# Attention whose probabilities meet v unnormalised: the row sums' reciprocals are applied to a pair's output

## The chip, the cores and the metric

The program runs on one core of a Trainium2 chip. The metric is the time of one execution in device microseconds, the median of three runs of the kernel before: 1122.89 us (1122.71 to 1123.68). Of the engines, PE (TensorE) multiplies and transposes, DVE (VectorE), ACT (ScalarE) and POOL (GpSimd) work elementwise, and SP (SyncE) issues the DMAs. Each takes its own instructions in order.

## The reference, cut to what matters

For 4 batches of 8 heads (S = 576 positions, D = 64 columns) attention with a decay is computed, and its output goes through two MLPs:

```
scores = q @ k.T / 8 + decay                    # masked above the diagonal
attn = exp(scores - max);  attn /= sum(attn) + 1e-9
x = attn @ v                                    # heads side by side: 2304 rows of 512
x = leaky(x @ w_in) @ w_out                     # 2048 wide
x = ((x @ w_a) * (x @ w_b)) @ w_o               # 1536 wide
```

## The kernel before

Attention runs in 34 steps `u`, one for each of the 32 heads and two to drain. In step `u` the scores of head `u` are made, head `u-1` is turned into P (its probabilities, transposed), and head `u-2` is multiplied with v (`LAG` = 2). Two heads, an even one and the odd one behind it, are a pair `g`: they fill the 128 partitions of x together. The first 512 query rows of a head are four row tiles `i` of 128 rows (names `sc_n_i`, 128 to 512 columns by the causal mask); the last 64 rows of both heads of a pair are one more tile, called r (`scr`, `sr`), made in the odd step.

The softmax of a tile is one DVE instruction (L354: mask, minimum) and one ACT instruction (L355: exp with the row sums `sm`). `rinv` makes `ri` = 32768/sum of the four tiles on DVE (`PSCALE` = 2^15).

There are two ways to P. Heads 0 to 9 (`NATIVE`) stay in float32: POOL multiplies each tile by `ri` in place (`p_hi`, L396), PE transposes it against the identity (`transposed`, L418), ACT or DVE copies the result out of PSUM, and `pv_whole` (L467) multiplies. Heads 10 to 31 are split in two float16 parts: POOL writes hi = s * ri (L409), DVE writes lo = s * ri - hi (L489), four tiles each, and a DMA transposes the tiles of a group ("lo": tiles 0 and 1, "hi": 2 and 3, "r") into `PT`. `pv` (L511 to L513) multiplies. Its output is put together by ACT (L544) and DVE (L545), and x is split into xh (ACT, L207) and xl (POOL, L551) for the first MLP.

In steps from 10 on, the first seven of sixteen column blocks of the first MLP (`mlp1a`, tiles h, g, y; `leaky` on ACT, DVE and POOL) are laid between attention's instructions, where the tables `even` and `odd` have an M. The y tiles are copied to `ys` (L686, two buffers) and stored to `ya_d`. Behind attention come the rest of the first MLP in passes (hb, ya) and the second MLP (a, b, o).

PSUM has eight banks: three for the MLP tiles and five (`at`) that go round among scores, transposes and pv. When attention has ended, they become four and four. The tables `even0`, `odd0` (first ten steps), `even` and `odd` give the order in which a step's parts are written; a scheduler then orders each engine's instructions by its own estimate.

Of the kernel before, what the change touches and what calls it, by code (L numbers as in the profile page):

```python
# [19 lines left out]
T = B * S  # L20
# [32 lines left out]
    eng0={'h3': 'pool', 'U': 'pool', 'h1': 'pool', 'e0': 'act', 'e2': 'act', 'e3': 'dve', 'e4': 'dve'},  # L53
    even0=['ri', 's3', 'T', 'p0', 'h2', 'h3', 's2', 'vs', 'h1', 's0', 'Q', 'M', 'M', 'M', 'M', 'l1', 'l2', 'h0', 's1', 'l0', 'l3', 'p1', 'V', 'po', 'W', 'M'],
    odd0=['ri', 'h3', 'h2', 'h0', 'R', 'h1', 'rr', 'M', 'Q', 'l2', 'T', 'l3', 'M', 's3', 'h4', 's2', 'l1', 'l0', 'M', 'M', 's1', 's0', 'p0', 'vs', 'p1', 'V', 'W', 'po', 'l4', 'M'],
# [21 lines left out]
def decay_attention_then_two_mlps(ctx, tc, q, k, v, f, w_in, w_out, alpha, w_a, w_b, w_o, out):  # L77
# [308 lines left out]
    def p_hi(n, i):  # L386

        g, o = GROUP[i]
        if n < NATIVE:
            s = s_view(n, i)  # L390
            ri = ap_["rir"][:, 0:1] if i == 4 else ap_["ri", n % 2][:, i:i + 1]
            e = eng(f"h{i}", "pool")
            if e is act:
                act.activation(s, s, AF.Copy, scale=ri)
            else:
                e.tensor_scalar(s, s, ri, 1.0, op0=ALU.mult, op1=ALU.mult)  # L396
            return
        if (n, g) not in p16:
            p16[n, g] = ap_["a"].tile(
                [128, GSIZE[g], 128], F16, tag=f"p16_{g}", name=f"p16_{n}_{g}", bufs=_P.get("p16", {}).get(g, 1),  # L400
            ), []
        t = p16[n, g][0][:, o:o + 2 * i + 2]
        s = s_view(n, i).rearrange("p (t n) -> p t n", n=128)
        ri = ap_["rir"][:, 0:1] if i == 4 else ap_["ri", n % 2][:, i:i + 1]
        e = eng(f"h{i}", "pool")
        if e is act:
            act.activation(t[:, 0::2, :], s, AF.Copy, scale=ri)
        else:
            e.tensor_scalar(t[:, 0::2, :], s, ri, 1.0, op0=ALU.mult, op1=ALU.mult)  # L409
        p16[n, i] = t, s, ri  # L410
# [73 lines left out]
    def p_lo(n, i):  # L484
        if n < NATIVE:
            return p_whole(n, i)
        t, s, ri = p16.pop((n, i))
        g, o = GROUP[i]
        eng(f"l{i}", "dve").scalar_tensor_tensor(t[:, 1::2, :], s, ri, t[:, 0::2, :], op0=ALU.mult, op1=ALU.subtract)  # L489
        whole, done_ = p16[n, g]  # L490
        done_.append(i)
        if g == "r" or len(done_) == 2:
            PT[n, g] = ap_["a2"].tile(
                [128, GSIZE[g], 128], F16, tag=f"PT_{g}", name=f"PT_{n}_{g}", bufs=2 if g == "r" else LAG,
            )
            sp.dma_start_transpose(out=PT[n, g], in_=whole.rearrange("p t n -> p (t n)"))
            del p16[n, g]

    def pv(u, c):
# [36 lines left out]
        x32 = xs[g, c]
        x = x32[p0:p0 + 64]
        if eng("x", "dve") is pool:
            y = ap_["a"].tile([128, 256 + SR], F32, tag="y", name=f"y_{u}_{c}")[p0:p0 + 64, :w]
            act.activation(x, ps_o[p0:p0 + 64, :w], AF.Copy, scale=1.0 / PSCALE)  # L540
            act.activation(y, ps_o[o0:o0 + 64, :w], AF.Copy, scale=1.0 / PSCALE)
            pool.tensor_tensor(x, x, y, op=ALU.add)
        else:
            act.activation(x, ps_o[o0:o0 + 64, :w], AF.Copy, scale=1.0 / PSCALE)  # L544
            dve.scalar_tensor_tensor(x, ps_o[p0:p0 + 64, :w], 1.0 / PSCALE, x, op0=ALU.mult, op1=ALU.add)  # L545
        if j == 0:
            return
        x_tiles(b)
        xh, xl = (x_[:, hp, h0:h0 + w] for x_ in X[b])
        dup(eng("xh", "act"), xh, x32)  # L550
        eng("xl", "pool").tensor_tensor(xl, x32, f32(xh), op=ALU.subtract)  # L551
# [388 lines left out]
```

## Time and profile before

| | |
|---|---|
| time, median of 3 runs | 1122.89 us (1122.71 to 1123.68) |
| the profiled execution | 1123.5 us, span 1121.5 us |
| PE busy | 1069.1 us, 95% of the span |
| DVE, ACT, POOL busy | 565.5, 524.4, 491.9 us |
| PE clock granted, mean | 0.993 |

The span is the time from the first to the last instruction of the profiled execution. A busy engine is one whose instructions run; a wait is idle time in front of an instruction, put down to what ended it. Neighbouring matmuls overlap, so the time from start to start is what one costs in a row of them.

### The profile page before, as it was taken

The page shows a single profiled execution, that of the slowest core. Times are in us where ns is not written, and L with a number is a line of the kernel's source. Part 1 is how long each engine was busy: PE and PEld are TensorE (multiplying, and loading weights), DVE is VectorE, ACT ScalarE, POOL GpSimd, SP SyncE. Part 2 cuts the span into 40 slices and gives each one's busy share as a digit, 9 for nine tenths or more (in the row PEclk, how much of TensorE's full clock was granted, in tenths as well). Part 3 has the DMA queues.
Part 4 walks back from the last instruction along what each step waited for, and adds up shares of the span by engine and source line. Part 5 has one row for each costly group of instructions (what it writes and reads, how often), then busy time and mean ns, then how long its engine had stood idle before and what let it go on. Part 6 is the DMA issues. An engine that isn't in the chain of part 4 may idle for free.

```text
span 1121.5 us, 18956 instructions
## 1 busy us (share of the span) xinstructions
PE 1069.1 (95%) x6663; PEld 1001.4 (89%) x6663; DVE 565.5 (50%) x1360; ACT 524.4 (47%) x1407; POOL 491.9 (44%) x627
## 2 busy tenths in 40 slices
PE   5899999998999999999998999999999999999997
PEld 3767888888888989999998999999999999999997
DVE  5688979888888286877588445400000000000000
ACT  5776776777777465666555444321121111211211
POOL 5555767667677355555556654311111111111111
PEclk9999999999999999999999999999999999999999
DMA  4645366767874764887778873120110100200000
GB/s 109 160 133 183 79 140 127 188 141 125 197 142 88 207 214 136 283 264 228 258 243 291 290 255 101 51 85 1 42 44 1 57 29 1 85 1 1 29 1 28
DMA packets 210771, 141.24 MB, mean 126 GB/s; under 512 B 138420, under 2 KB 196788, under 8 KB 210676
## 3 DMA queue, kind: packets, MB, share of 16 engines
q1 hardware_dynamic: 210676, 140.03, 44.7%
q8 instruction: 52, 0.85, 0.3%
q14 instruction: 43, 0.35, 0.1%
HBM read 88.30 MB, written 33.65 MB: 109 GB/s over the span
## 4 chain that ended last, share of the span: by engine, by line
PE 60%; DVE 4%; DMA 2%; POOL 1%; issue 1%; ACT 1%; SPq 0%; DVEq 0%; POOLq 0%; ACTq 0%
PE a L646 5%; PE b L646 5%; PE a L645 5%; PE b L644 5%; PE b L645 5%; PE a L644 5%; PE o L644 4%; PE o L645 4%; PE o L646 4%; PE ya L645 3%; PE ya L644 3%; PE hb L644 3%; PE hb L646 3%; PE ya L646 3%; PE hb L645 3%
## 5 line engine op out<-in xcount | busy, mean ns | idle before, releaser
L910 DVE TENSOR_TENSOR as<-b,as 128x384 f32<-128x384 f32 x72 | 40.1, 557 | 367.6 <-PE b L646 366.7
L912 POOL TENSOR_TENSOR gg<-as,gg 128x384 fp32r<-128x384 f32 x72 | 73.2, 1017 | 334.9 <-ACT gg L911 334.9
L909 ACT COPY as<-a 128x384 f32<-128x384 f32 x72 | 34.6, 480 | 170.9 <-PE a L646 170.8
L911 ACT CAST gg<-as 128x384 fp32r<-128x384 f32 x72 | 36.9, 513 | 152.4 <-DVE as L910 152.3
L639 DVE SCALAR_TENSOR_TENSOR lt<-lu,nal,lt 128x288 f32<-128x288 f32 (+1 forms) x110 | 75.6, 688 | 54.5 <-ACT lt L638 53.9
L646 PE MATMUL a<-yh,w_a 128*128 128x384 f32 x288 | 97.2, 338 | 0.0
L646 PE MATMUL b<-yh,w_b 128*128 128x384 f32 x288 | 97.1, 337 | 0.0
L645 PE MATMUL a<-yl,w_a 128*128 128x384 f32 x288 | 97.1, 337 | 0.0
L644 PE MATMUL b<-yh,w_b 128*128 128x384 f32 x288 | 97.1, 337 | 0.0
L645 PE MATMUL b<-yl,w_b 128*128 128x384 f32 x288 | 97.1, 337 | 0.0
L644 PE MATMUL a<-yh,w_a 128*128 128x384 f32 x288 | 97.1, 337 | 0.0
L644 PE MATMUL o<-w_o,gg 128*128 128x512 f32 x216 | 84.4, 391 | 0.0
L645 PE MATMUL o<-w_o,gg 128*128 128x512 f32 x216 | 84.4, 391 | 0.0
L646 PE MATMUL o<-w_o,gg 128*128 128x512 f32 x216 | 84.2, 391 | 0.0
L355 ACT ACTIVATE s<-s,nm 128x512 f32<-128x512 f32 (+3 forms) x128 | 71.5, 560 | 22.9 <-DVE nm L354 22.2
L641 POOL TENSOR_TENSOR gb<-lt,gb 128x384 fp32r<-128x384 f32 x54 | 56.5, 1047 | 41.8 <-ACT gb L640 36.0
L645 PE MATMUL ya<-gb,w_out 128*128 128x384 f32 x216 | 73.3, 339 | 1.0 <-POOL gb L641 1.0
L644 PE MATMUL ya<-gb,w_out 128*128 128x384 f32 x216 | 71.3, 340 | 2.4 <-DVE yl L837 2.3
L646 PE MATMUL ya<-gb,w_out 128*128 128x384 f32 x216 | 72.9, 337 | 0.0
L645 PE MATMUL y<-g,w_out 128*128 128x288 f32 x224 | 69.2, 312 | 3.4 <-POOL g L641 3.4
L644 PE MATMUL y<-g,w_out 128*128 128x288 f32 x224 | 67.1, 312 | 2.5 <-ACT g L640 2.5
L644 PE MATMUL h<-xh,w_in 128*128 128x288 f32 x224 | 67.3, 303 | 1.5 <-ACT lt L638 1.1
(185 smaller groups left out, 3228.1 us busy)
## 6 DMA issues: line engine op xcount, KB each, us to landing
yl<-ya_d SPq DMA_DIRECT2D x48, 192.0 KB
wr_in<-in_moe_w_in SPq DMA_DIRECT2D x32, 256.0 KB
wr_out<-in_moe_w_out SPq DMA_DIRECT2D x32, 256.0 KB
wr_a<-in_moe_w_a SPq DMA_DIRECT2D x24, 256.0 KB
wr_b<-in_moe_w_b SPq DMA_DIRECT2D x24, 256.0 KB
wr_o<-in_moe_w_out SPq DMA_DIRECT2D x24, 256.0 KB
qkn<-in_q SPq DMA_DIRECT2D x64, 72.0 KB
qkn<-in_k SPq DMA_DIRECT2D x64, 72.0 KB
```

The costliest lines, as they stand in the source:

```text
L355: act.activation(s, s, AF.Exp, bias=nm, scale=-1.0, accum_out=sm)
L639: dve.scalar_tensor_tensor(t, u, nal[:, fi:fi + 1], t, op0=ALU.mult, op1=ALU.add)
L641: pool.tensor_tensor(gl, t, f32(gh), op=ALU.subtract)
L644: pe.matmul(o, lh, rh, start=start, stop=False)
L645: pe.matmul(o, lh, rl, start=False, stop=False)
L646: pe.matmul(o, ll, rh, start=False, stop=stop)
L909: act.copy(asb[:, :n], aps[:, :n])
L910: dve.tensor_tensor(asb[:, :n], bps[:, :n], asb[:, :n], op=ALU.mult)
L911: ap_["last"] = act.copy(g[:, 0, :n], asb[:, :n]).ins
L912: pool.tensor_tensor(g[:, 1, :n], asb[:, :n], f32(g[:, 0, :n]), op=ALU.subtract)
```

## The change

P is no longer multiplied by the reciprocal of its sum in row tiles 0 to 3. The reciprocals of a pair are spread by a DVE copy over 64 columns per head (`rinv_pair`), turned into rows by four PE transposes of 128x128 into one `at` bank (`rinv_rows`, new entry `rl` of the odd tables), copied by ACT into the one buffer `rrow`, and x of the pair is multiplied by `rrow`: in native heads as DVE reads the PSUM tile, in the others by one POOL instruction of 128x576 in x's only buffer. xh and xl are made once per pair, 576 columns wide. Tile r keeps its multiplication by `rir`. hi and lo are made by two instructions per head instead of four (`SPAN`: tiles 0 and 1 lie side by side as "lo", 384 columns, and tiles 2 and 3 as "hi", 896 columns), and native tiles 0 to 3 have no multiplication. `ys` goes from two buffers to one. The tables change; of them a line stands here.

```
-    odd="ri h3 h2 h0 R rr vs h1 M Q l2 T l3 s2 M h4 s3 l1 M M s1 l0 s0 p0 p1 V W po l4 M".split(),
+    odd="rl h1 h0 ri R rr vs M Q l1 T s2 M h4 s3 l0 M M s1 s0 p0 p1 V W po l4 M".split(),
...
+        ap_["rrow"] = a.tile([128, S], F32, name="rrow")
+        pool.memset(ap_["rrow"][:, ST:], 1.0 / PSCALE)
...
+    def rinv(sm, ri, scale):
+        dve.tensor_scalar(sm, sm, 1e-9, scale, op0=ALU.add, op1=ALU.mult)
+        if len(ri.shape) == 3:
+            dve.reciprocal(sm, sm)
+            dve.tensor_copy(ri, sm.unsqueeze(2).broadcast_to([128, 4, D]))
...
+    def rinv_pair(n):
+        g, j = divmod(n, 2)
+        if g not in RI:
+            RI[g] = ap_["a"].tile([128, 4, 2, D], F32, tag="ri", name=f"ri_{g}")
+        return RI[g][:, :, j]
+
+    def rinv_rows(g):
+        o = bank(f"rrow_{g}")
+        ri = RI.pop(g)
+        for i in range(4):
+            w = ri[:, i].rearrange("p j d -> p (j d)")
+            pe.transpose(o[:, 128 * i:128 * i + 128], w, ap_["ident"])
+        act.copy(ap_["rrow"][:, 0:ST], o)
...
+    SPAN = {0: ("lo", 0, 384), 1: ("hi", 384, 1280), 4: ("r", 0, 640)}
...
+    def p_hi(n, r):
         if n < NATIVE:
+            if r == 4:
+                s = ap_["sr"]
+                pool.tensor_scalar(s, s, ap_["rir"][:, 0:1], 1.0, op0=ALU.mult, op1=ALU.mult)
             return
+        g, s, scale = p_parts(n, r)
+        t = p16[n, r] = ap_["a"].tile([128, GSIZE[g], 128], F16, tag=f"p16_{g}", name=f"p16_{n}_{g}")
+        eng(f"h{r}", "pool").tensor_scalar(t[:, 0::2], s, scale, 1.0, op0=ALU.mult, op1=ALU.mult)
...
-        act.activation(xh, ps_o[:, :w], AF.Copy, scale=1.0 / PSCALE)
-        dve.scalar_tensor_tensor(xl, ps_o[:, :w], 1.0 / PSCALE, f32(xh), op0=ALU.mult, op1=ALU.subtract)
+        cs = slice(256 * c, 256 * c + w)
+        dve.tensor_tensor(x_pair(g)[:, cs], ps_o[:, :w], ap_["rrow"][:, cs], op=ALU.mult)
+        if c == 1:
+            x_out(g)
+
+    def x_pair(g):
+        if g not in xs:
+            xs[g] = ap_["a"].tile([128, S], F32, tag="x32", name=f"x32_{g}")
+        return xs[g]
+
+    def x_out(g):
...
+        dup(eng("xh", "act"), xh, x)
+        eng("xl", "pool").tensor_tensor(xl, x, f32(xh), op=ALU.subtract)
...
+        act.copy(x, ps_o[o0:o0 + 64, :w])
+        dve.tensor_tensor(x, ps_o[p0:p0 + 64, :w], x, op=ALU.add)
+        if j == 1 and c == 1:
+            eng("xr", "pool").tensor_tensor(xs[g], xs[g], ap_["rrow"], op=ALU.mult)
+            x_out(g)
...
-                ys = mp["t"].tile([128, HB], F32, tag="ys", name=f"ys_{b}_{a0}_{e_}")
+                ys = mp["t"].tile([128, HB], F32, tag="ys", bufs=1, name=f"ys_{b}_{a0}_{e_}")
```

On DVE, where head 30 is turned into P (step 31; `p16_30` are its float16 parts, `x32_14` the output of pair 14, `lt_2` a leaky of the MLP), there stood before:

```order
L377 TENSOR_SCALAR sm_0_152<-sm_0_152 128x4
L378 RECIPROCAL ri_0_153<-sm_0_152 128x4
L545 SCALAR_TENSOR_TENSOR x32_14_0_4991<-pv_28_0_4984,x32_14_0_4991 64x256
L489 SCALAR_TENSOR_TENSOR p16_30_hi_5049<-s_0_150,ri_0_153,p16_30_hi_5049 128x4x128
L639 SCALAR_TENSOR_TENSOR lt_2_5027<-lu_2_5028,nal_73,lt_2_5027 128x288
L545 SCALAR_TENSOR_TENSOR x32_14_1_5022<-pv_28_1_4994,x32_14_1_5022 64x320
L489 SCALAR_TENSOR_TENSOR p16_30_hi_5049<-s_0_150,ri_0_153,p16_30_hi_5049 128x3x128
L489 SCALAR_TENSOR_TENSOR p16_30_lo_5052<-s_0_150,ri_0_153,p16_30_lo_5052 128x128
L489 SCALAR_TENSOR_TENSOR p16_30_lo_5052<-s_0_150,ri_0_153,p16_30_lo_5052 128x2x128
```

and now, with the spread copy as its last row:

```order
L379 TENSOR_SCALAR sm_0_152<-sm_0_152 128x4
L381 RECIPROCAL sm_0_152<-sm_0_152 128x4
L563 TENSOR_TENSOR x32_14_4987<-pv_28_0_4980,x32_14_4987 64x256
L520 SCALAR_TENSOR_TENSOR p16_30_hi_5048<-s_0_150,p16_30_hi_5048 128x7x128
L663 SCALAR_TENSOR_TENSOR lt_2_5022<-lu_2_5023,nal_73,lt_2_5022 128x288
L520 SCALAR_TENSOR_TENSOR p16_30_lo_5050<-s_0_150,p16_30_lo_5050 128x3x128
L563 TENSOR_TENSOR x32_14_4987<-pv_28_1_4990,x32_14_4987 64x320
L382 COPY ri_15_5052<-sm_0_152 128x4x64
```

Four lo instructions have become two, and one copy of 256 columns has come behind them.

On POOL at the end of attention (`p16_31`: head 31, `g_2_288`: the MLP tile of batch 2 that the y matmuls read, `xl_3`: batch 3), there stood before:

```order
L641 TENSOR_TENSOR g_2_288_4868<-lt_5_5130,g_2_288_4868 128x288
L409 TENSOR_SCALAR p16_31_hi_5222<-s_1_159,ri_1_162 128x4x128
L409 TENSOR_SCALAR p16_31_hi_5222<-s_1_159,ri_1_162 128x3x128
L409 TENSOR_SCALAR p16_31_lo_5225<-s_1_159,ri_1_162 128x128
L409 TENSOR_SCALAR p16_31_lo_5225<-s_1_159,ri_1_162 128x2x128
L551 TENSOR_TENSOR xl_3_4475<-x32_14_0_4991,xh_3_4474 128x256
L551 TENSOR_TENSOR xl_3_4475<-x32_14_1_5022,xh_3_4474 128x320
L641 TENSOR_TENSOR g_2_288_4868<-lt_6_5209,g_2_288_4868 128x288
L551 TENSOR_TENSOR xl_3_4475<-x32_15_0_5274,xh_3_4474 128x256
L551 TENSOR_TENSOR xl_3_4475<-x32_15_1_5305,xh_3_4474 128x320
```

and now:

```order
L427 TENSOR_SCALAR p16_31_hi_5218<-s_1_158 128x7x128
L665 TENSOR_TENSOR g_2_288_4867<-lt_4_5112,g_2_288_4867 128x288
L427 TENSOR_SCALAR p16_31_lo_5220<-s_1_158 128x3x128
L665 TENSOR_TENSOR g_2_288_4867<-lt_5_5132,g_2_288_4867 128x288
L565 TENSOR_TENSOR x32_14_4987<-x32_14_4987,rrow_163 128x576
L665 TENSOR_TENSOR g_2_288_4867<-lt_6_5207,g_2_288_4867 128x288
L503 TENSOR_TENSOR xl_3_4507<-x32_14_4987,xh_3_4506 128x576
L565 TENSOR_TENSOR x32_15_5269<-x32_15_5269,rrow_163 128x576
L503 TENSOR_TENSOR xl_3_4507<-x32_15_5269,xh_3_4506 128x576
```

Between the last two g instructions (lt_5 and lt_6) there were six instructions, and now there is one.

On ACT, where the last y tiles of `mlp1a` are copied out and the first tiles of the next pass (`hb_0_7`) begin, there stands now, as before but for one row of weights:

```order
L710 COPY ys_3_288_0_6057<-y_3_288_0_6013 128x288
L132 CAST w_out11_5817<-wx_out11_2_5829 128x256
L710 COPY ys_3_288_1_6060<-y_3_288_1_6014 128x288
L710 COPY ys_3_288_2_6107<-y_3_288_2_6063 128x288
L710 COPY ys_3_288_3_6110<-y_3_288_3_6064 128x288
L661 ACTIVATE lu_7_6148<-hb_0_7_6133 128x384
```

All four copies stand in front of the first leaky of the pass; with one buffer three of them follow a store.

## Rows read from the trace of the kernel before

**Rows 1.** The page's first part: busy time, share of the span, instructions.
```profile
PE 1069.1 (95%) x6663; PEld 1001.4 (89%) x6663; DVE 565.5 (50%) x1360; ACT 524.4 (47%) x1407; POOL 491.9 (44%) x627
```

**Rows 2.** Windows by stage: length; busy PE, PEld, DVE, ACT, POOL; clock, DMA.
```profile
28.00:112.00 84.00, 76.46 (x466) 60.67 (x465) 65.44 (x211) 61.47 (x185) 45.31 (x67) 1.00 0.56 159
112.00:364.00 252.00, 235.68 (x2017) 219.02 (x2015) 218.73 (x582) 186.41 (x558) 173.15 (x247) 1.00 0.66 136
364.00:448.00 84.00, 78.57 (x546) 76.63 (x547) 50.80 (x98) 44.02 (x121) 39.61 (x46) 0.94 0.62 186
448.00:1121.00 673.00, 663.99 (x3579) 635.48 (x3577) 215.97 (x423) 216.35 (x504) 218.58 (x232) 1.00 0.34 111
```

**Rows 3.** PE's waits, 20 to 118 us: total us, times, longest.
```profile
PE sc L338 <- ACT PT_hi L207: 3.1, 3, 1.7
...
PE tp L418 <- POOL s L396: 1.1, 3, 0.5
```

**Rows 4.** PE's waits, 118 to 364 us.
```profile
PE pv L511 <- DVE nm L354: 4.3, 9, 1.0
PE sc L341 <- DVE x L545: 3.2, 5, 1.0
PE sc L341 <- DVE nm L354: 3.1, 7, 0.6
```

**Rows 5.** Timeline of PE near 100 us: start, us, instruction, count.
```profile
100.37 0.49 PE L418 MATMUL tp<-ident,s 128*128 128x128 f32 x3
100.70 0.66 PE L307 MATMUL tqk<-ident,qkn 96*128 96x96 f32 x6
```

**Rows 6.** DVE by form, 0 to 440 us: busy us, mean ns | idle before.
```profile
L489 DVE SCALAR_TENSOR_TENSOR p_hi<-s,ri,p_hi 128x512 f16<-128x512 f32 x22 | 23.1, 1050 | 6.4 <-POOL p_hi L409 6.3
...
L489 DVE SCALAR_TENSOR_TENSOR p_hi<-s,ri,p_hi 128x384 f16<-128x384 f32 x22 | 16.8, 762 | 0.2
L489 DVE SCALAR_TENSOR_TENSOR p_lo<-s,ri,p_lo 128x256 f16<-128x256 f32 x22 | 15.4, 699 | 0.1
...
L489 DVE SCALAR_TENSOR_TENSOR p_lo<-s,ri,p_lo 128x128 f16<-128x128 f32 x22 | 13.9, 631 | 0.3
...
L129 DVE TENSOR_SCALAR wx_in<-wx_in 128x256 int32<-128x256 int32 x24 | 8.5, 355 | 11.2 <-ACT wx_in L127 11.2
...
L209 DVE COPY PT_r<-tp 128x256 f32<-128x256 f32 x5 | 2.1, 412 | 0.0
```

**Rows 7.** POOL's instructions of L396: count, ns min/median/max, first and last start.
```profile
L396 POOL TENSOR_SCALAR s<-s,ri x40: 368/597/948, 20.0 to 116.0; 128x512 f32<-128x512 f32 x10, 128x384 f32<-128x384 f32 x10, 128x128 f32<-128x128 f32 x10, 128x256 f32<-128x256 f32 x10
```

**Rows 8.** POOL by form, 0 to 440 us: busy us, mean ns | idle before.
```profile
L551 POOL TENSOR_TENSOR xl<-x,xh 128x320 fp32r<-128x320 f32 x11 | 10.1, 915 | 1.3 <-ACT xh L207 1.0
L551 POOL TENSOR_TENSOR xl<-x,xh 128x256 fp32r<-128x256 f32 x11 | 9.5, 868 | 11.3 <-ACT xh L207 11.2
```

**Rows 9.** Timeline of POOL, 361 to 368.6 us.
```profile
361.99 1.26 POOL L409 TENSOR_SCALAR p_hi<-s,ri 128x512 f16<-128x512 f32 x2
363.21 1.46 POOL L409 TENSOR_SCALAR p_lo<-s,ri 128x128 f16<-128x128 f32 x2
364.64 1.89 POOL L551 TENSOR_TENSOR xl<-x,xh 128x256 fp32r<-128x256 f32 x2
366.49 0.97 POOL L641 TENSOR_TENSOR g<-lt,g 128x288 fp32r<-128x288 f32 x1
```

**Rows 10.** Timeline of PE, 365.5 to 368.8 us, with the idle time before.
```profile
367.51 0.40 PE L645 MATMUL y<-g,w_out 128*128 128x288 f32 x1 [1.72 <-POOL g L641]
```

**Rows 11.** Window behind that wait, columns as in rows 2.
```profile
368.50:371.80 3.30, 3.30 (x16) 3.30 (x15) 0.48 (x1) 0.83 (x2) 0.00 (x0) 0.50 0.94 112
```

**Rows 12.** Timeline of ACT, 426 to 446 us.
```profile
431.06 0.69 ACT L686 COPY ys<-y 128x288 f32<-128x288 f32 x2
434.68 0.79 ACT L686 COPY ys<-y 128x288 f32<-128x288 f32 x2 [2.93 <-DMA ya_d<-ys]
435.36 0.50 ACT L637 ACTIVATE lu<-hb 128x384 f32<-128x384 f32 x1
```

More of the change, by code (lines that the diff above doesn't have):

```diff
@@ L52 @@
     es=10,
[L53 to L55 removed]
+    eng0={'U': 'pool', 'e0': 'act', 'e2': 'act', 'e3': 'dve', 'e4': 'dve'},
+    even0="l3 s3 T l2 ri p0 s2 vs l1 s0 Q l0 s1 p1 V po W".split(),
+    odd0="l3 R l2 rl ri rr Q T s3 l1 l0 s2 s1 h4 s0 p0 vs p1 V W po l4".split(),
 )
@@ L237, in attention_setup @@
             ap_["s", i] = a.tile([128, 1280], F32, tag=f"s_{i}", name=f"s_{i}")
-            for nm in ("nm", "sm", "ri"):
+            for nm in ("nm", "sm"):
                 ap_[nm, i] = a.tile([128, 4], F32, tag=f"{nm}_{i}", name=f"{nm}_{i}")
@@ L374, in softmax_rest @@
         act.activation(s[:, :S], s[:, :S], AF.Exp, bias=nm[:, 0:1], scale=-1.0, accum_out=sm[:, 0:1])
-    def rinv(sm, ri):
-        dve.tensor_scalar(sm, sm, 1e-9, 1.0 / PSCALE, op0=ALU.add, op1=ALU.mult)
-        dve.reciprocal(ri, sm)
+    def rinv(sm, ri, scale):
[3 more added lines that the diff above has]
+            dve.tensor_copy(ri, sm.unsqueeze(2).broadcast_to([128, 4, D]))
+        else:
+            dve.reciprocal(ri, sm)
+    RI = {}
+    def rinv_pair(n):
[10 more added lines that the diff above has]
+        act.copy(ap_["rrow"][:, 0:ST], o)
     PT = {}
@@ L384, in decay_attention_then_two_mlps, with p_parts @@
     GSIZE = {"lo": 6, "hi": 14, "r": 2 * NQ}
-    def p_hi(n, i):
-        g, o = GROUP[i]
-        if n < NATIVE:
[L390 to L396, printed above, removed]
-            return
[L398 to L410, printed above, removed]
+    SPAN = {0: ("lo", 0, 384), 1: ("hi", 384, 1280), 4: ("r", 0, 640)}
+    def p_parts(n, r):
+        g, a0, a1 = SPAN[r]
+        s = (ap_["sr"] if r == 4 else ap_["s", n % 2])[:, a0:a1]
+        return g, s.rearrange("p (t n) -> p t n", n=128), ap_["rir"][:, 0:1] if r == 4 else PSCALE
+    def p_hi(n, r):
+        if n < NATIVE:
+            if r == 4:
+                s = ap_["sr"]
+                pool.tensor_scalar(s, s, ap_["rir"][:, 0:1], 1.0, op0=ALU.mult, op1=ALU.mult)
+            return
+        g, s, scale = p_parts(n, r)
+        t = p16[n, r] = ap_["a"].tile([128, GSIZE[g], 128], F16, tag=f"p16_{g}", name=f"p16_{n}_{g}")
+        eng(f"h{r}", "pool").tensor_scalar(t[:, 0::2], s, scale, 1.0, op0=ALU.mult, op1=ALU.mult)
     P32 = {}
@@ L482, in x_tiles, with p_lo @@
             )
-    def p_lo(n, i):
+    def p_lo(n, r):
         if n < NATIVE:
[L486 to L497, printed above, removed]
+            if r == 4:
+                p_whole(n, 4)
+            return
+        t = p16.pop((n, r))
+        g, s, scale = p_parts(n, r)
+        eng(f"l{r}", "dve").scalar_tensor_tensor(t[:, 1::2], s, scale, t[:, 0::2], op0=ALU.mult, op1=ALU.subtract)
+        PT[n, g] = ap_["a2"].tile(
+            [128, GSIZE[g], 128], F16, tag=f"PT_{g}", name=f"PT_{n}_{g}", bufs=2 if g == "r" else LAG,
+        )
+        sp.dma_start_transpose(out=PT[n, g], in_=t.rearrange("p t n -> p (t n)"))
     def pv(u, c):
@@ L531, in pv @@
                 passes(ps_o[:, 256:w], t, ptr[:, 2 * t, qs], ptr[:, 2 * t + 1, qs], t == 0, t == NQ - 1)
-        b, hp = divmod(g, NP)
-        if (g, c) not in xs:
-            xs[g, c] = ap_["a"].tile([128, w], F32, tag=f"x32_{c}", name=f"x32_{g}_{c}")
         p0, o0 = 64 * j, 64 * (1 - j)
[L536 to L551, printed above, removed]
+        cs = slice(h0, h0 + w)
+        x = x_pair(g)[p0:p0 + 64, cs]
+        act.copy(x, ps_o[o0:o0 + 64, :w])
[3 more added lines that the diff above has]
+            x_out(g)
     xs = {}
@@ L595, in attention @@
                     if cur(u - 1):
-                        rinv(ap_["sm", (u - 1) % 2], ap_["ri", (u - 1) % 2])
+                        sm = ap_["sm", (u - 1) % 2]
+                        rinv(sm, rinv_pair(u - 1), 1.0 if u - 1 < NATIVE else PSCALE)
+                elif op == "rl":
+                    if u > 1 and cur(u - 2):
+                        rinv_rows(u // 2 - 1)
                 elif op in ("h4", "l4"):
@@ L602, in attention @@
                     if cur(u - 1):
-                        (p_hi if a == "h" else p_lo)(u - 1, int(i))
+                        if u - 1 >= NATIVE:
+                            (p_hi if a == "h" else p_lo)(u - 1, int(i))
+                        elif a == "l":
+                            late = u >= _P.get("es", 0)
+                            for i in ((1, 2, 3) if i == "1" else (0,)) if late else (int(i),):
+                                p_whole(u - 1, i)
                 elif op == "R":
```

11 lines of the change are left out of this document (6 added, 5 removed).

## The prediction

> **What bounds the kernel now.** I read the busy shares first. PE is busy for 95% of the span and the next engine, DVE, for 50% [rows 1], so the end is set by PE's work plus PE's waits. Second came the stages [rows 2]. Behind 448 us PE is busy for 664 of 673 us, and the change touches nothing there: that part keeps its length and only begins earlier or later. What can move lies in the first 448 us. There PE is idle for 84 - 76.5 = 7.5 us while the native heads run, for 252 - 235.7 = 16.3 us beside the split heads, and for 84 - 78.6 = 5.4 us where attention ends and the first MLP's last blocks run, and in this last stage the granted clock is also only 0.94 [rows 2]. Third came what ended PE's waits. Beside native heads it is most of all a PSUM tile that ACT has not yet copied out, and in three places POOL's multiplication of P [rows 3]. Beside split heads it is DVE: the pv and score matmuls wait for an `at` bank until DVE has read it, 4.3 + 3.2 + 3.1 = 10.6 us of the 16.3 [rows 4]. DVE is busy for 218.7 of 252 us in that stage, 87% [rows 2]; a bank comes free late because DVE takes its instructions in order. Last I looked at the single worst wait at the end of attention [rows 9 to 11].
>
> The terms below are changes of the profiled execution's own time, 1123.5 us for a span of 1121.5 us; it lies 0.6 us above the median of the runs, 1122.89 us, to which I apply the sum.
>
> **A. The transposes that are added.** Four per pair and 16 pairs make 64 transposes of 128x128. Three such take 0.33 us from start to start (100.37 to 100.70) [rows 5], so one is 0.11 us and all are 64 x 0.11 = 7.0 us of PE, which is the bound. Hidden are only those that fall where PE would have waited: it waits for 24 us of 336 in the two stages, 7% [rows 2]. I take +6.5 us; the ends are 0 (all in waits; work is added, so no gain) and +7.0.
>
> **B. Native heads.** POOL loses 40 multiplications, 0.60 us in the median [rows 7], and a transpose no longer waits for the last of a head's row sums, two small DVE instructions and POOL's queue: it can go as soon as its tile's exp is done. The 1.1 us of PE's waits for POOL [rows 3] go for certain. What is next is the copy out of PSUM, on which 3.1 us were waited [rows 3]; with the transposes earlier, and tile 3's in front, ACT and DVE get these copies at times when PE has other work. Against it stand, per pair, one ACT copy of 512 columns and two DVE copies of 256. I take -4 us: the 1.1, and most of 3.1. The ends are -7.5 (all of the stage's idle time) and +2 (ACT's new copy, about half a microsecond for each of 5 pairs by the shorter copies of [rows 12], always in front of a bank).
>
> **C. Split heads.** Four lo instructions of one head take 1.05 + 0.76 + 0.70 + 0.63 = 3.14 us [rows 6]. The rise from 128 to 512 columns is 0.42 us, 1.09 ns for a column, so one of 896 columns should take 1.05 + 384 x 1.09 ns = 1.47 us, and with the 384-column one 2.23 us: 0.91 us less. The copy that spreads the reciprocals, 256 float32 columns, lies between 0.36 us (256 columns inside SBUF) and 0.41 us (out of PSUM) [rows 6]; I take 0.36, as it lies in SBUF. Multiplying x by 1/32768 (L545) becomes a plain add at the same price. So DVE is relieved by 0.55 us a head, 22 x 0.55 = 12 us of 218.7: its idle time rises from 33 to 45 us. POOL's four hi instructions of a head are 1.26 + 1.46 = 2.7 us [rows 9]; two save about 1 us of it, as the fixed part goes twice. It gets the multiplication by `rrow`, 576 columns: the xl of 320 takes 0.92 and that of 256 0.87 us [rows 8], so between 1.1 (their slope) and 1.8 us (both together); I take 1.4, between them, and the one wider xl saves some 0.4 of that again. POOL thus has about 1 us less per pair. If waits for a queue go with one over its idle time, 10.6 us become 10.6 x 33/45 = 7.8; the hi instructions also no longer wait for `ri`, which lets the lo instructions start together rather than at the moment when the next scores want DVE. I take -5 us, about half of the waits. The ends are -10.6 and +4: the bank that `rrow` takes is the 19th use of five banks per pair where there were 18, and the lo instruction of 1.47 us blocks DVE longer at a stretch than one of 1.05.
>
> At this place a rule speaks against the change. The four sizes show that the 128-column instruction takes 0.63 us and the 256-column one hardly more, 0.70 [rows 6], while POOL is at work beside them. The Trainium skill, GPSIMD Engine Reference, 1. Specifications, says that GpSimd shares its SBUF interfaces with VectorE and that it contends with VectorE instructions that have two SBUF inputs; these have two, and the trace agrees as far as the short one is so dear. By that rule the new POOL multiplication lengthens what runs beside it on DVE, and fewer instructions save less than their count. What this would make of the sum is the second rival.
>
> **D. The end of attention.** Before its g instruction at 366.49 us POOL works through four hi and two xl instructions without a gap [rows 9], and PE's y matmul waits 1.72 us for that g [rows 10]. Just behind, the clock is granted at 0.50 for the 3.3 us that the window shows [rows 11], which costs 1.65 us more. The order now has one instruction there in place of six. Next are the x of the last two pairs: a pair's x gets POOL's multiplication (1.4 us) ahead of xh, and xl is 576 wide, some 2.3 us more until the next batch's first matmuls have all their x; PE has 21 y matmuls and nine h matmuls that do not need the last pair to put there. I take -3 us, with -3.4 and +2.3 as ends.
>
> **E. One ys buffer.** The third copy of the last four waited 2.93 us for the store of the first [rows 12]: with two buffers that happens once, with one it happens three times. Between, PE has the first four tiles of the pass, 12 matmuls each, at 664/3579 = 0.19 us [rows 2] 2.2 us a tile, and each of these needs a bank that a ys copy must free. A copy every 3.6 us (434.68 - 431.06) against a tile every 2.2 us would cost up to 3 x 1.4 = 4.2 us; a store that has the queue to itself should be quicker than two together. In front of attention's end the y tiles lie further apart than a store takes, but for the first two of a block, five times. I take +2 us in all, ends 0 and +6.7 (two more waits of 2.93, and 0.8 of copies behind them).
>
> **Sum.** 6.5 - 4 - 5 - 3 + 2 = -3.5 us: 1122.9 - 3.5 = 1119.4 us.
>
> **The rivals.**
> *Slower: PE pays the transposes and no bank comes free sooner.* The place is the split-head stage. If the DVE waits there stay at over 8 us in all, because a bank's release hangs on DVE's order and not on its load, then C is 0 and B only the 1.1: 7.0 - 1.1 + 0 - 3 + 2 = +4.9, 1127.8 us. For it: the same DVE instructions (mask, x, T) still stand between a bank and its reuse, and one bank use is added. Against it: DVE's 87%, at which 12 us are much. It decides from A + E = 8.5 us, which the other terms must outweigh.
> *No change: the contention moves.* The new POOL multiplication and the longer lo instructions keep each other waiting, and C is -1: 6.5 - 4 - 1 - 3 + 2 = +0.5, 1123.4 us. For it: the dear short instructions above. Against: POOL has less work in sum.
> *Much faster: the waits go.* B and C reach most of their far ends, -6 and -9: 6.5 - 6 - 9 - 3.4 + 1 = -10.9, 1112 us. For it: nothing else than DVE is named in the three rows of [rows 4]; against: PE is at 94% there, and any in-order engine keeps some.
>
> **How the numbers follow.** The forecast has 0.32, with 1116 to 1120.6 as its own range; much faster 0.15; no change 0.25; slower 0.28. A difference under 0.2%, 2.2 us, can't be told from none in a measurement of this kernel. So faster is 0.32 + 0.15 = 0.47, same 0.25, slower 0.28. The range for 8 in 10 is 1110 to 1131: it leaves out about a third of the much-faster case and those slower outcomes in which E and the end of attention go wrong together with C.
>
> **What the profile would show.** A: 64 transposes at 0.11 us, PE busy beside split heads up by about 5 us. B: no wait of a transpose for POOL, fewer than 7 us idle between 28 us and the end of the native heads. C: lo instructions of about 1.5 and 0.8 us, a spread copy under 0.4 us, and PE's waits for DVE at 5 to 6 us. D: the y wait at the end of attention gone and no half clock there. E: three ys copies that each wait 2 to 3 us for a store, behind the last h block. I am wrong if the DVE waits stay above 8 us, if the x of a pair, in its one buffer, makes ACT or PE wait in every pair, or if the native stage gets longer.

## The result, and the profile after

The changed kernel takes 1138.3 us in the median (1135.6 to 1139.8), the kernel before in the same runs 1123.3: a ratio of 1.0129 (1.0113 to 1.0144), slower by some 15 us. The forecast was 1119.4 us with a range of 1110 to 1131: wrong in sign, and the time lies outside of the range. The rival "PE pays" is nearest, but at 1127.8 it explains a third.

The busy shares of the changed kernel, against [rows 1]:

```profile
PE 1075.5 (95%) x6727; PEld 1008.6 (89%) x6727; DVE 564.5 (50%) x1348; ACT 526.3 (46%) x1407; POOL 469.9 (41%) x549
```

PE has its 64 instructions and 6.4 us more. POOL lost 22 us and DVE 1 us of 565. The stages of the changed kernel, columns as in [rows 2]:

```profile
28.00:112.00 84.00, 76.55 (x471) 61.06 (x469) 64.35 (x213) 63.08 (x185) 30.72 (x38) 1.00 0.49 134
112.00:364.00 252.00, 234.68 (x2003) 221.04 (x2001) 211.39 (x552) 180.88 (x542) 160.04 (x196) 0.99 0.70 143
364.00:448.00 84.00, 72.64 (x558) 68.81 (x557) 49.38 (x97) 43.30 (x121) 40.84 (x44) 0.99 0.55 172
...
448.00:1136.00 688.00, 676.90 (x3647) 647.88 (x3646) 224.24 (x439) 224.09 (x524) 224.10 (x238) 1.00 0.34 111
```

By B, C and D, PE's idle time and half clocks should have fallen by 12 us. The idle time is 7.5 us beside native heads as before, 17.3 beside split heads (16.3 before), and 11.4 at the end of attention (5.4 before). So added work is paid in full and nothing comes back. These windows lie at fixed times, while the changed kernel falls behind in its work from window to window; windows cut at the same place of the work stand under "The balance". PE's waits, first beside native heads (20 to 118 us), against [rows 3], then beside split heads (118 to 364), against [rows 4] (total us, times, longest):

```profile
PE sc L340 <- ACT N L207: 3.4, 4, 2.0
PE pvw L484 <- ACT PT_lo L207: 1.5, 1, 1.5
PE pvw L484 <- ACT lt L662: 0.8, 1, 0.8
```

```profile
PE h L669 <- POOL xl L503: 5.1, 2, 3.9
PE sc L343 <- DVE nm L356: 3.4, 4, 1.9
PE tqk L309 <- DVE x L563: 1.9, 2, 1.6
PE sc L343 <- DVE x L563: 1.6, 2, 1.0
...
PE pv L538 <- DVE nm L356: 0.8, 3, 0.3
```

The old waits did go: POOL's multiplication in the native heads, and pv's 4.3 us behind DVE (0.8 now). Others took their places: ACT's copies of q and k (N) in the native heads, POOL's xl in the split heads.

The largest single wait, on POOL and on PE of the changed kernel (start, us, instruction, idle before it and what ended it):

```profile
300.34 1.44 POOL L565 TENSOR_TENSOR x<-x,rrow 128x576 f32<-128x576 f32 x1 [2.20 <-ACT T L323]
301.86 0.94 POOL L211 TENSOR_SCALAR U<-U 64x288 fp32r<-64x288 f32 x2
306.96 0.72 POOL L290 TENSOR_TENSOR vs<-vs 128x320 f32<-128x320 f32 x1 [4.16 <-DMA vs<-in_v]
307.63 1.40 POOL L503 TENSOR_TENSOR xl<-x,xh 128x576 fp32r<-128x576 f32 x1
```

```profile
309.08 0.48 PE L669 MATMUL h<-xl,w_in 128*128 128x288 f32 x1 [3.94 <-POOL xl L503]
```

POOL is free at 302.8, and ACT has made xh by 302.5 (it starts at 301.81 and takes 0.67 us), but in POOL's order the next head's vs, which waits for a load, stands between x's multiplication and xl. PE waits 3.9 us, and the window behind it shows the clock granted at about half:

```profile
309.00:312.40 3.40, 3.31 (x20) 3.17 (x21) 2.17 (x3) 2.35 (x7) 2.09 (x4) 0.54 1.08 336
```

The ys chain behind attention, on ACT of the changed kernel, against [rows 12]:

```profile
444.05 0.40 ACT L710 COPY ys<-y 128x288 f32<-128x288 f32 x1 [3.34 <-DMA ya_d<-ys]
446.33 0.40 ACT L710 COPY ys<-y 128x288 f32<-128x288 f32 x1 [1.88 <-DMA ya_d<-ys]
450.77 0.40 ACT L710 COPY ys<-y 128x288 f32<-128x288 f32 x1 [4.04 <-DMA ya_d<-ys]
```

Three waits for a store, as step E said; the half clock stands here too (0.53 from 446.0 to 449.4).

### The profile page after: what moved, and what is told of

Same layout as the page of the kernel before. It is cut to its first block, busy times and chain, and to the rows that moved or that the text cites. A ratio compares the mean times of both kernels' runs of the same rounds, so it can differ in the third digit from the quotient of the medians.

```text
span 1136.6 us, 19011 instructions
## 1 busy us (share of the span) xinstructions
PE 1075.5 (95%) x6727; PEld 1008.6 (89%) x6727; DVE 564.5 (50%) x1348; ACT 526.3 (46%) x1407; POOL 469.9 (41%) x549
## 4 chain that ended last, share of the span: by engine, by line
PE 66%; DVE 12%; DMA 8%; ACT 5%; issue 4%; POOL 3%; SPq 1%; POOLq 0%; ACTq 0%; DVEq 0%
PE a L670 4%; PE a L669 4%; PE b L670 4%; PE b L669 4%; PE b L668 4%; PE a L668 4%; PE o L668 4%; PE o L669 4%; PE o L670 4%; DMA wr_in<-in_moe_w_in 3%; PE ya L669 3%; PE ya L670 3%; PE ya L668 3%; PE hb L668 2%; PE hb L670 2%
## 5 line engine op out<-in xcount | busy, mean ns | idle before, releaser
L663 DVE SCALAR_TENSOR_TENSOR lt<-lu,nal,lt 128x288 f32<-128x288 f32 (+1 forms) x110 | 78.8, 718 | 60.2 <-ACT lt L662 59.5
L357 ACT ACTIVATE s<-s,nm 128x512 f32<-128x512 f32 (+3 forms) x128 | 71.4, 561 | 17.6 <-DVE nm L356 16.9
L668 PE MATMUL y<-g,w_out 128*128 128x288 f32 x224 | 66.8, 307 | 6.3 <-ACT g L664 5.8
L669 PE MATMUL h<-xl,w_in 128*128 128x288 f32 x224 | 67.1, 301 | 5.1 <-POOL xl L503 5.1
```

Source lines behind the costliest of these rows:

```text
L357: act.activation(s, s, AF.Exp, bias=nm, scale=-1.0, accum_out=sm)
L663: dve.scalar_tensor_tensor(t, u, nal[:, fi:fi + 1], t, op0=ALU.mult, op1=ALU.add)
L668: pe.matmul(o, lh, rh, start=start, stop=False)
L669: pe.matmul(o, lh, rl, start=False, stop=False)
```

## The experiments

Each time is a median, with its ratio to the kernel before in the same runs. "Points" below are thousandths of 1123 us, 1.1 us each; "repairs" are the edits of e1 and e7.

**e1.** `ys` takes `mp["ys"]`, a pool of two buffers made when attention's space is free.


> The changed kernel, in which the last two blocks behind attention have a pool of their own with two ys buffers; attention keeps its single one. Theory: behind attention the third copy of four waits for a store three times, and this is the 7.8 us by which PE's idle time between 420 and 448 us grew (11.1 in place of 3.3). Then the time falls from 1138.3 to 1130.5, and PE's waits for ys are near 2 us. Rival: PE is held there by the g of the leaky ahead, which ends late because attention ends differently; then the time stays within 2 us of 1138.3.


1133.3 us (1128.9 to 1136.1), 1.0092 (1.0071 to 1.0112): 3.7 points, 4.2 us, came back. Its PE does the same as the changed kernel's, in the same order, up to the pass behind attention. **e2**, the opposite, `bufs=1` for `ys` in the kernel before:


> The kernel before, with one ys buffer in place of two and nothing else. Theory: the single buffer costs 8 us wherever it stands: 1123.3 + 8 = 1131. Rival: the +2 us of the prediction's step E, 1125, with the rest of the changed kernel's loss there made by the change of attention.


1128.5 us, 1.0046 (1.0034 to 1.0058): 5.2 us lost. ACT of e2 shows the same three waits:

```profile
437.36 0.40 ACT L686 COPY ys<-y 128x288 f32<-128x288 f32 x1 [3.31 <-DMA ya_d<-ys]
439.64 0.40 ACT L686 COPY ys<-y 128x288 f32<-128x288 f32 x1 [1.89 <-DMA ya_d<-ys]
441.92 0.40 ACT L686 COPY ys<-y 128x288 f32<-128x288 f32 x1 [1.88 <-DMA ya_d<-ys]
```

The single buffer costs 4 to 5 us in either kernel: more than 2, and less than the 7.8 that I then read off the idle time.

**e3.** `rinv_rows` only drops its tile; `rrow` is a constant.


> The changed kernel without the 64 transposes of the reciprocals, their bank and ACT's copy (rrow holds a constant, so x is not divided by the sums). Theory: all of the transposes lie on PE's path: 7 us less, 1131.3. Rival 1: they fall in waits, 1137 to 1138. Rival 2: the bank and the ACT copy cost as well, more than 9 us less, under 1129.


1125.1 us, 1.0015 (1.0005 to 1.0025): 12.8 us less. This looked like rival 2.

**e4.**
```
+            with tc.issue_after(ap_["xl"]):
                 eng(f"v{i}", "pool").tensor_tensor(vs[:, :, i + 1], ...
```


> The changed kernel, with POOL's two vs instructions of the next head placed behind xl of the pair; in the changed kernel the first of them stands between x's multiplication and xl in every pair, and waits there for the load of v. Theory: the two h waits for xl (5.4 us) and the half clock behind the longer one (1.7 us) go, 1138.3 - 7 = 1131; at least 3 us less if vs is then late for pv. Rival: POOL's three steps for x (multiplication, xh, xl) are long by themselves, and less than 2 us goes.


1134.8 us, 1.0103 (1.0090 to 1.0116): 2.9 us less, between the theory and the rival. No wait of pv for vs stands in its list, so the theory's reason for a smaller gain isn't what happened. The wait for xl is gone from the list of PE's waits beside split heads, but its first rows now read:

```profile
PE sc L344 <- DVE x L564: 4.4, 4, 1.8
PE sc L344 <- DVE nm L357: 2.5, 4, 0.8
PE sc L344 <- DVE nmr L373: 1.7, 2, 0.8
```

**e5.** Native heads as in the kernel before, split heads as changed, ys as in e1 (one head's reciprocals were those of another; e11 mends it).


> The change in the split heads alone: the ten native heads are as before (POOL multiplies P by the reciprocals, no transposes of reciprocals, xh and xl from PSUM, the old tables of the first ten steps); two ys buffers behind attention as in e1, 1133.3. Theory: the native part brings nothing, its five pairs of transposes cost 2.2 us or, by the price that e3 gave for all 16 (13 us), 4 us, and little comes back: 1129 to 1131. Rival: the native part is the good one, as step B has it (4 us gained against 2.2): 1135.


1122.1 us, 0.9988 (0.9977 to 0.9999): 11.7 us under e1, more than the theory.

**e6.** `for i in range(1)` in `rinv_rows`, and a copy that repeats it.


> The changed kernel with one of the four transposes of a pair; ACT copies this one's 128 columns four times, so bank and copy stay (three of four row tiles get wrong divisors). Theory: what e3 saved beyond PE's 7 us is owed to the bank and to ACT's copy; then 48 x 0.11 = 5.3 us go, 1133. Rival: the transposes cost more than their PE time, by when they come; then three quarters of the 13 us go, 1128.5.


1120.5 us, 0.9971 (0.9959 to 0.9983): 17.7 us less. Both expectations miss: with a quarter of the transposes it is faster than e3 with none. Taking away less cannot save more by its own weight, so these edits do something else as well: the scheduler reorders the engines behind each edit (1106 of PE's 6974 rows moved in e6, 2506 in e3; 75 in e1). e9 and e10 measure that.

**e7.** `act.copy(ri, ...)` in place of `dve.tensor_copy(ri, ...)` in `rinv`.


> The changed kernel with the copy that spreads the reciprocals on ACT in place of DVE. On DVE it takes 0.49 us in the mean and up to 1.5 us where POOL works beside it, 10.7 us of 22 copies beside split heads. Theory: DVE's release is what the banks wait for, so 2 to 4 us are won, 1134.5 to 1136.5. Rival: DVE's load doesn't decide, and ACT's queue becomes longer in front of PE's banks: no gain, 1138 to 1141.


1131.4 us, 1.0063 (1.0047 to 1.0079): 7.4 us less, more than the theory's 2 to 4.

**e8.** The transposes, of the identity, in the kernel before.


> The kernel before with step A alone laid on top: in each odd step four transposes of the identity into one at bank and an ACT copy of it to a buffer that nothing reads. Theory: PE's 7 us and, through bank and ACT copy, some 6 more, as e3 gave it: 1123 + 13 = 1136. Rival: 7 us, 1130; the other 6 of e3 would then belong to what waits for rrow.


1131.7 us, 1.0071 (1.0058 to 1.0084): 8.0 us, near the rival's 7. In sum step A costs its PE time and little more, in this one order; the 12.8 and 17.7 us of e3 and e6 are not its price.

**e9, e10.** `rates=[0, 1.01, 1.01, 1.01, ...` in both kernels: same work, other order.


> The changed kernel with the rates at which MLP work is laid beside steps 8 to 31 raised from 1 to 1.01: the same instructions, but the scheduler puts them in another order on every engine (1353 of 6974 rows of PE move). Theory: the time of one and the same work depends on the order by several us, so that part of the 15 us and of what e3, e5, e6 and e7 saved is not owed to the instructions they touch: 1130 to 1136, over 2 us off 1138.3. Rival: the order matters by under 1.5 us, 1137 to 1140, and these runs can be read at their face.


1134.6 us, 1.0103 (1.0089 to 1.0117): 2.9 us less.


> The same edit of the rates in the kernel before (2176 of 6953 rows of PE move). Theory: its order is the best of many, another one costs 2 to 8 us, 1125 to 1131. Rival: within 1.5 us of 1123.4.


1119.5 us, 0.9974 (0.9963 to 0.9985): 2.9 us less, where the theory had the shipped order best. So the 2.9 us of e4, which reorders too, can't be told from an effect of order.

**e11.** e5 with head 9's reciprocals in their place.


> e5 with the two small DVE instructions of head 9's reciprocals put in front of its POOL multiplications, which had used those of head 7 there; nothing else. Theory: the native part was what cost, and this stays at e5's 1122, 0 to 4 us under the kernel before. Rival: e5 owed its time to a lucky order; then this other one (the PE rows of a step move) gives 1126 to 1131.


1128.0 us, 1.0043 (1.0028 to 1.0057). Two tiny instructions moved, and 6.2 us went: the rival. e5's order was a lucky one.

**e12.** e11 with e7's edit.


> e11 with the spread copy on ACT in place of DVE, as in e7. Theory: DVE's 10.7 us of copies, which POOL lengthens, are what e7 won by (7 us): 3 to 7 us under e11, 1115 to 1119. Rival: e7's gain was one of order; within 2 us of e11 on either side.


1118.5 us, 0.9960 (0.9947 to 0.9972): 9.3 us under e11, more than the 7 at most that I expected.

**e13.** `dve.reciprocal(ri, sm.unsqueeze(2).broadcast_to([128, 4, D]))`, no copy.


> The changed kernel in which DVE's reciprocal writes the 256 spread columns itself, and the copy is gone. In the traces the reciprocal of 4 columns takes 0.176 us with POOL at work and without, where the copy rises from 0.28 to 0.69 us in the mean. Theory: what counts is that POOL holds up the copy; then this wins what e7 won, 4 to 8 us, 1130.5 to 1134.5, with every such reciprocal of one duration. Rival 1: DVE's load alone counts; a reciprocal of 256 columns (0.28 us of copy and 0.18) saves 0.2 us a head, 1 to 2 us, 1136.5 to 1137.5. Rival 2: e7's gain was its order, any result within 4 us of 1138.3.


1152.5 us, 1.0265 (1.0248 to 1.0281): 15.3 us more, and no theory had that. DVE by form, 112 to 364 us of e13 (busy, mean ns):

```profile
L381 DVE RECIPROCAL ri<-sm 128x256 f32<-128x256 f32 x21 | 36.6, 1743 | 0.2
```

A reciprocal of 256 columns takes 1.74 us, one of 4 takes 0.18: I had priced it like a copy. The test that it was to be failed, but it gives the price of DVE's load. Over 32 heads DVE has 32 x 1.743 = 55.8 us of it in place of 15.0 of copies and 5.6 of small reciprocals, 35 us more, and the time rose by 15.3: 0.43 us for each us on DVE. e7 took the 15.0 us of copies off DVE and won 7.4: 0.49. Both edits reorder, and e7's gives ACT the copies, so these are rough rates.

**e14.** The whole change with e7's and e1's edits.


> The whole change with the spread copy on ACT (e7) and two ys buffers behind attention (e1). Theory: the two are independent, 1138.3 - 6.9 - 5.1 = 1126; against e12 (1118.5), which has the same two and the native heads of before, the native part then costs 7 or 8 us. Rival: most of the native part's price in e5 was order; then this lies within 3 us of e12, at 1121.5 or less.


1125.4 us, 1.0027 (1.0016 to 1.0038), 7.5 us above e12: the theory. The two repairs add up, and the native part costs.

**e15, e16.** `rates` at 0.99: a third order of both kernels.


> The kernel before with the rates of steps 8 to 31 at 0.99 in place of 1: the same work, a third order (2712 of 6953 rows of PE move). Theory: orders scatter by 3 to 4 us about a middle near 1122: 1118 to 1127. Rival: the order shipped is a bad or a good one by more than that: outside of it.


1118.4 us, 0.9960 (0.9944 to 0.9976).


> The same edit in the changed kernel (2620 of 6974 rows of PE move). Theory: the middle of its orders lies near 1136, so this is at 1132 to 1140, and no order of the changed kernel comes within 8 us of the kernel before. Rival: the order shipped was a bad one and this falls under 1130.


1135.6 us, 1.0114 (1.0095 to 1.0133). Both as the theory had it. Three orders of the kernel before lie at 1.0000, 0.9974, 0.9960, three of the changed one at 1.0129, 1.0103, 1.0114. The means differ by 13.7 points, 15.4 us, and no order of one comes near one of the other: the loss belongs to the change, and single runs that reorder are known to some 3 us at best (6 between e5 and e11). In e9, e10, e15 and e16 PE, ACT, DVE and POOL start in the shipped order; the first instruction that differs comes at 134 to 143 us on PE and later on the others, behind the native heads. So they try other orders of the split heads, and none of the native heads.

**e17, e18.** e12 with the two other rates.


> e12 with the rates of steps 8 to 31 at 1.01, as in e10: the same work in another order (2419 of 6965 rows of PE move). Theory: the split heads' two instructions and the end of attention win about what their 44 transposes cost, so the orders of e12 lie about those of the kernel before, 1118 to 1123. Rival: the split part with both repairs is better by 3 us or more in every order: 1113 to 1117.


1117.8 us, 0.9943 (0.9928 to 0.9958): the fastest kernel here, ahead of both.


> e12 with the rates at 0.99, as in e15: a third order (3992 of 6965 rows of PE move). Theory: 1118 to 1123 as for e17. Rival: 1113 to 1117.


1120.8 us, 0.9968 (0.9954 to 0.9983). The mean of e12's orders is 0.9957, of the kernel before's 0.9978: 2.4 us, which three orders each don't settle.

## Why the prediction was wrong, step by step

The steps that failed are B and C, the gains that were to come from POOL's and DVE's load: PE's waits in the native and the split heads are no shorter than before. B took it that the waits for ACT's copies would go with those for POOL, and they grew; C's relief of DVE, 0.55 us a head, was 0.30 by the durations. D's gain was cancelled, and E was put too low. No single step makes the 15 us.

**A, the transposes (+6.5): right.** PE is busy 6.4 us longer with 64 of them, and e8 gives 8.0.

**E, one ys buffer (+2): mechanism right, size wrong.** Three waits, as said, but 4.0 (e7 to e14), 4.2 (e1) and 5.2 us (e2). I had credited the matmuls between the copies against them and assumed quicker stores; two of the three took longer than the store in [rows 12]. PE shows it directly: its first 60 matmuls from the first hb on take 16.0 us in the changed kernel and 12.0 in e1.

**C, the split heads (-5): the step that failed is DVE's relief of 0.55 us a head.** DVE by form, 112 to 364 us of the changed kernel:

```profile
L663 DVE SCALAR_TENSOR_TENSOR lt<-lu,nal,lt 128x288 f32<-128x288 f32 x39 | 27.7, 714 | 2.1 <-ACT lt L662 1.8
L520 DVE SCALAR_TENSOR_TENSOR p_hi<-s,p_hi 128x896 f16<-128x896 f32 x21 | 26.6, 1265 | 9.6 <-POOL p_hi L427 9.5
...
L520 DVE SCALAR_TENSOR_TENSOR p_lo<-s,p_lo 128x384 f16<-128x384 f32 x21 | 15.0, 713 | 0.1
...
L382 DVE COPY ri<-sm 128x256 f32<-128x256 f32 x22 | 10.7, 488 | 0.2
...
L379 DVE TENSOR_SCALAR sm<-sm 128x4 f32<-128x4 f32 x22 | 10.3, 469 | 9.0 <-ACT s L357 8.9
```

and two rows of the same view of the kernel before:

```profile
L639 DVE SCALAR_TENSOR_TENSOR lt<-lu,nal,lt 128x288 f32<-128x288 f32 x41 | 26.1, 638 | 2.8 <-ACT lt L638 2.4
...
L377 DVE TENSOR_SCALAR sm<-sm 128x4 f32<-128x4 f32 x23 | 5.2, 228 | 9.7 <-ACT s L355 9.4
```

The lo instructions take 1.98 us where I had 2.23, better than said: against 3.14 before [rows 6] 1.16 us saved a head. But the copy takes 0.49, not 0.36; the TENSOR_SCALAR of 4 columns, which the change doesn't touch, has doubled; and the leaky, some 1.8 a head, is 0.08 us longer. Net 1.16 - 0.49 - 0.24 - 0.13 = 0.30 us a head, little over half of what I had. Why? DVE and POOL of the changed kernel side by side:

```profile
139.49 1.51 DVE L382 COPY ri<-sm 128x256 f32<-128x256 f32 x1
...
214.59 1.08 DVE L379 TENSOR_SCALAR sm<-sm 128x4 f32<-128x4 f32 x1 [1.03 <-ACT s L357]
215.70 0.18 DVE L381 RECIPROCAL sm<-sm 128x4 f32<-128x4 f32 x1
```

```profile
139.12 1.74 POOL L503 TENSOR_TENSOR xl<-x,xh 128x576 fp32r<-128x576 f32 x1
140.82 0.76 POOL L290 TENSOR_TENSOR vs<-vs 128x320 f32<-128x320 f32 x1
...
214.25 1.40 POOL L503 TENSOR_TENSOR xl<-x,xh 128x576 fp32r<-128x576 f32 x1
```

Both DVE instructions end within 0.15 us of POOL's xl. Sorted by whether a POOL instruction was running when they began (112 to 440 us): the copy 0.28 us without (12 of them) and 0.69 with (11), the TENSOR_SCALAR 0.16 (4) and 0.55 (19), but the reciprocal 0.177 and 0.175, and x (L563, its 256 columns), which reads PSUM, 0.42 both ways. The Trainium skill, SBUF — State Buffer, Who interferes with whom, says that a copy or tensor_scalar between SBUF tiles can take the pair of ports that VectorE shares with GpSimd, for the whole instruction, and that the other then waits; the durations here agree, for these two and for the reciprocal, which is in no such list. Before the change POOL's hi waited for `ri`, so POOL mostly stood idle while DVE began to make it (at 18 of 23 TENSOR_SCALARs, against 4 of 23 now). Freed from `ri`, POOL runs at just that time. The prediction named hi's freedom as a gain, and weighed contention only for the lo instructions. Its rate, about half a us of time for one of DVE, agrees with e7 and e13. With the copy on ACT (405 ns) 7.4, 7.3 (e1 to e14) and 9.3 us come back. Not all of this is POOL's doing: of the 15.0 us of copies 32 x 0.28 = 9.0 are there without POOL, so by the same rate some 3 us are its hold-up and the rest the copy's own load on DVE. That is an estimate; e13, which was to part the two, didn't.

At the same work ("The balance") DVE is busy 4.8 us less beside the split heads in the shipped orders, and 1.3 in the mean of three orders each, of the 12 that I took. At that rate 1 to 2 us were left to win, and PE's idle time rose by about 1 instead. POOL's chain to xl (multiplication 1.54, xh 0.67, xl 1.51 us in the mean, with vs between) doesn't explain it: in e9, the same work in another order, PE waits for no xl beside split heads, and that kernel lies 11.6 us over the one before. PE's 5.1 us for xl belong to the shipped order. What else took them stays open.

**D, the end of attention (-3): the waits named are gone, the gain didn't come.** The 1.72 us for POOL's g and the half clock behind [rows 10, 11] are gone; the mean clock of the stage is 0.99 against 0.94. In their place PE waits for ACT's g:

```profile
374.78 0.40 PE L668 MATMUL y<-g,w_out 128*128 128x288 f32 x1 [1.66 <-ACT g L664]
```

And half clocks came at 142, 309 and 446 us instead, 1.7 us each, as many as left (one at 368 us, and 7 us in a row from 416.5, worth two). From the last pv to the first hb matmul, 55.3 us before and 56.3 now in the mean of three orders each, nothing was won.

**B, the native heads (-4): the gain failed, and against the old native heads there is a loss.** PE's idle time up to the end of the native heads is 21.6 us before and 21.9 now ("The balance"). Three pairs of kernels price the whole native part, with its tables, at 5.5 (e11 to e1), 7.5 (e12 to e14) and 11.7 us (e5 to e1, with e5's lucky order); 2.2 of it are its transposes. I said that the transposes' earlier start lets the waits go, and allowed ACT 2 us at worst. But PE now waits for what ACT does in a row. ACT of the changed kernel, and PE behind it:

```profile
43.17 0.56 ACT L402 COPY rrow<-rrow 128x512 f32<-128x512 f32 x1
...
45.96 0.43 ACT L127 ACTIVATE wx_in<-wr_in 128x256 f32<-128x256 f32 x1 [1.07 <-DMA wr_in<-in_moe_w_in]
46.41 0.80 ACT L207 COPY N<-tqk 64x288 f32<-64x288 f32 x2
47.12 0.67 ACT L207 CAST xh<-x 128x576 fp32r<-128x576 f32 x1
```

```profile
47.27 0.49 PE L340 MATMUL sc<-N 128*128 128x128 f32 x2 [1.96 <-ACT N L207]
```

The scores now wait for N, which stands behind a weight's part that waits for its load. With both repairs (e14) it is rrow's own copy for which PE waits most, where e12, with the old native heads, has POOL:

```profile
PE sc L340 <- ACT rrow L402: 2.5, 2, 1.5
PE pvw L484 <- ACT PT_lo L207: 2.3, 3, 1.4
```

```profile
PE tp L435 <- POOL s L423: 3.4, 4, 1.8
PE sc L340 <- ACT PT_hi L207: 1.3, 2, 0.9
```

So POOL's waits are exchanged for ACT's. Of the 6.4 us between the spans of e14 and e12, 4.8 are lost by the last native multiplication, which starts at 132.0 and 127.2 us: PE is busy 2.2 us longer up to there, as the transposes are priced, and idle 2.6 us longer. The rest goes beside the split heads; behind the last pv the two differ by 0.7 us, the other way. All of this is for one order and one table of the native steps, new in the change; another table was not tried, so it is open whether ACT's row or its place in the table costs the 2.6 us.

**The rivals.** "PE pays" was right on PE and wrong on the banks: the three waits of [rows 4] fell from 10.6 to 5.8 us, with tqk's new one 7.7. "No change" had a mechanism that is there, contention that moves, but looked for it between POOL's multiplication and the lo instructions; its 4 us are near the estimate of 3 for the copy. Of the signs of being wrong, DVE's waits stayed under 8 us and x made ACT wait in four places, not in every pair; only the longer native stage showed. No case let B, C and D all bring nothing while E went wrong, so the range ended too low.

**The balance.** The start of the last native multiplication (`pvw`) and that of the last pv part each run at the same place of its work. The three parts of the kernel before, columns as in [rows 2]:

```profile
0.00:126.70 126.70, 105.08 (x627) 83.64 (x628) 93.94 (x301) 91.34 (x271) 71.12 (x121) 1.00 0.51 135
126.70:376.00 249.30, 231.70 (x2008) 215.35 (x2007) 208.91 (x546) 175.54 (x521) 166.08 (x233) 0.99 0.68 140
376.00:1121.50 745.50, 732.35 (x4037) 702.43 (x4033) 262.63 (x514) 257.56 (x616) 254.74 (x274) 0.99 0.37 120
```

and of the changed kernel:

```profile
0.00:130.60 130.60, 108.72 (x646) 86.58 (x647) 97.42 (x309) 91.64 (x266) 55.25 (x85) 1.00 0.50 132
130.60:383.50 252.90, 234.46 (x2054) 220.91 (x2054) 204.09 (x526) 177.43 (x526) 158.16 (x190) 0.99 0.69 137
383.50:1136.60 753.10, 732.29 (x4036) 701.08 (x4032) 263.02 (x514) 257.24 (x616) 256.45 (x274) 0.99 0.36 119
```

PE is busy 3.6 us longer in the first part, 2.8 in the second, and as long as before in the third: this is A, whose transposes lie in the first two. PE's idle time goes from 21.6 to 21.9, from 17.6 to 18.4 and from 13.2 to 20.8 us. So B brought none of its 4 us and C none of its 5, and behind attention, where D and E together should have won 1, 7.7 are lost. With A's 6.4 that makes the 15.1 us between the spans. Of the 7.7, E is 5.2 (in e14, with two ys buffers, PE is idle for 15.6 us there), and D lost 2.4 where it should have won 3.

PE's idle times by part, with the other orders, in which a few y matmuls lie on the other side of the second cut:

| | native heads | split heads | behind |
|---|---|---|---|
| before: shipped, e10, e15 | 21.6, 20.1, 22.7 | 17.6, 15.6, 14.7 | 13.2, 16.3, 13.6 |
| changed: shipped, e9, e16 | 21.9, 22.1, 22.4 | 18.4, 15.8, 17.0 | 20.8, 20.6, 17.6 |
| whole, both repairs: e14 | 23.2 | 12.6 | 15.6 |
| split part, both repairs: e12, e17, e18 | 20.7, 21.5, 21.3 | 12.1, 11.9, 11.3 | 16.0, 15.5, 17.4 |

That the native and the split heads won nothing holds in all three orders, and so does a loss behind; the sizes there are known to some 3 us. With the copy on ACT the split heads do win 3 to 5 us of idle time, near C's 5. Why e3 and e6 saved 12.8 and 17.7 us by removing transposes that cost 8 stays open: order by itself has shown up to 6. In e6 PE is idle for 11.7 us beside the split heads (112 to 364 us) against 17.3, and 4.7 of the difference are its waits for xl, which e9 lost too by order alone.

## What to carry to other kernels

When an edit frees one engine from waiting on another, ask what the two then do at the same time: here POOL, no longer waiting for DVE's reciprocals, held up the copy that made them, and the copy belonged on ACT. A wait removed in an in-order queue is worth little until the next one is priced: in the native heads POOL's went to ACT. Where a scheduler reorders everything behind an edit, time the same work in a few orders before reading a difference of under 4 to 6 us as the edit's. And look in both traces for the time at which one and the same instruction starts: it shows which stage has lost time, which windows at fixed times don't, as they hold different work.

## What the runs showed of the hardware

A DVE reciprocal costs 6.2 ns a column ((1743 - 176) / 252), six times a DVE copy of 256 columns in 0.28 us, and POOL at work doesn't lengthen it (1.742 and 1.745 us). DVE instructions of which an input lies in PSUM (mask, x, the splits of q and k) had the same duration to 3% with POOL at work and without, in the kernel before and in the changed one.
